# Attention and a squared-relu feed-forward: who issues the last stores, batch three's queries by the DMA crossbar, and another order

## The chip, the cores and the metric

The kernel runs on one core of a Trainium2 chip. The metric is the device time of one execution in microseconds. Besides it there is one profiled execution, with its own time, from which all rows below come.

## The reference

```python
q, k, v: (8, 8, 576, 64); p: (8, 8, 32, 64)              # batch, heads, sequence, head dimension
def sm_attn(qq, kk, vv):
    s = matmul(qq, kk.T) / sqrt(64)
    a = exp(s - max(s)); a = a / (sum(a) + 1e-9)
    return matmul(a, vv)
p_packed = sm_attn(p, k, v)                              # 32 packed rows per head
attn = sm_attn(q, p_packed, p_packed)                    # (8, 8, 576, 64)
x = attn.transpose(0, 2, 1, 3).reshape(4608, 512)
out = square(maximum(x @ w_in, 0)) @ w_out               # (512, 2048), (2048, 512): float32 (4608, 512)
```

## The kernel before, in words

**Work.** The eight batches (b) go through the same steps. k, q and v are loaded in halves of four heads (Lk, Lq, Lv; GpSimd issues these loads, which also cast to bf16). k is transposed by DVE (Tk), v is put in place by DVE (Cv, two halves, each after all four pieces of Lv of that batch). S1 gives the scores of the packed rows, PV the packed rows (XT takes them out of PSUM: a copy, a reciprocal, and two small copies into `pq`, `pq_part` or `pq_swap`). M multiplies the packed rows with `w_in`, so that the second attention and the first feed-forward matmul become one (R: 16 matmul steps per batch, each followed by a relu on ACT or DVE; F1: squares into `gT`). S2 and N are the scores and the normalisation of the second attention; S2 needs the transposed queries `qT`.

**Queries.** In batches that aren't in `XBAR`, DVE transposes the queries (`tr_q`, line 275). In batches in `XBAR`, SP issues a DMA transpose of each half from SBUF to SBUF (Tq, `xbar_q`, line 281), `s2_x` takes 16 matmuls in place of 32 (line 413 in place of 430), `pq_swap` stands for `pq_part`, and the output rows of that batch are stored in another order. `qT` has two buffers.

**Second feed-forward matmul.** The 36 output tiles of 128 tokens (F2) are done one by one up to tile 6 and for tile 35; tiles 7 to 34 go in seven groups of four (`GROUPS`), named by their first tile. A group computes the four tiles' halves by seven products of sums and differences (F2.g.n.kk: product n of 1 to 7, eight steps kk), with WS the sums of `gT` on DVE and `prod_out` the copies and additions from PSUM into `o_sb`. Products 1, 3, 5 and 7 share one bank, so product 3 starts when product 1 has been copied out. `o_sb` has three buffers: a new one can be written when all stores of the tile pair three back have landed.

**Stores.** ST.t (or ST.g.6 for tiles g and g+1, ST.g.7 for g+2 and g+3) stores a tile in two pieces of two DMAs, each of 32 rows. Every piece may go by SP, from tile 8 on by GpSimd, and from tile 31 on by ACT:

```python
for e, us, eng in (("SP", 0.86, nc.sync), ("POOL", 1.0, Q), ("ACT", 0.86, A))
if e == "SP" or t >= (8 if e == "POOL" else 31)]
```

**Order.** Steps are cut into pieces. `ORDER` is a packed list with one number for each piece: which of its allowed engines does it, and its place in one list over all engines. `Plan.run` unpacks it and issues the pieces in that order; each engine then works its own pieces strictly in that order, and a piece whose data isn't there holds all behind it on its engine. This includes SP, which issues stores and crossbar transposes, and GpSimd, which issues loads and stores. `FILL` gives, for some early steps, how many idle matmuls TensorE does ahead of them (`keep_clock`). The names used below (Lv.6.0.0, Cv.6.0, XT.5, ST.4) are step names: kind, batch or tile, and piece. Line 1024 is the barrier behind the kernel, line 541 the stores, 226 to 247 the loads of q, k and v, 172 and 170 copies by DVE and ACT.

Of the kernel before, what the change touches and what calls it, by code (L numbers as in the profile page):

```python
# [76 lines left out]
ORDER = (
    'c-jrt17j5m7y!`EVd3s-)mm;DtJSit)t23smR2phwrsm)+qP}nw)x(#I0rx=2_%A~kP{3NLssyC<d6rFfg6H>At7V}FQkRy;0t~b0;wS*l!E+F'
    '0IESQ2!cvb1}Z``C<$dD9I8Vd=mQO)IgEx*&<z$sD`*chpfc2iE>Ig9!VstcRiQ16fU$5G2E$0$3QZsqCPGgb0IOjEEQM>Z9M-`tm;jUEEKGyh'
    'a0xcUPIv@2;2tEvy>JNLzzH}9-{B5C1t&g+*N_HZzz4{Tf<9OQ^I#$DitpeH1fv^MV_p0Tf1wzb#!A==t6(i0h&8c3j>kaEjV*C8uEmp>5wl@q'  # L80
    'oPi5)54ORMxEkl<ay)=f@eL9+$F?{ZH{x!*hVStQ`cX~_p_cRtKcX*9!CAN&SK<~thei%6Lf`NYrls_hjj9n-BFamXXcn!cxwM!zQYy+smFW>a'
    '!w)!?rqB|q%}sd#XQ3c!K-IY}_vQf3#QC`ix8k8ZgXYsZy2RJ{F_+=0+?p$KICtjJG=XMPDo)2a_zK_Q_gsieazif0<+wR#<Gfs%GjdKY$_NS$'
    'AV>iIkPb39(mMhn3uJQ?0w=h@11F&<6oXgr9!B6;{EEM^EA^*j?B=PwjO$5PNdYM#4Wx1eIL<>NOo=-%DV?QBoEdUJFSr6Vurpr5JNOS%6R`3k'
    'KE;(KO7cQ^Xbdet(Tg*2116*jRFSGuZ>mXkr~_@GU38ST(>}UD-}oOVl0S@+N|K6O0>vd>36kuP8}dOBC<uk21eAtyPzA!Eh9eYi!hN_4Pv9B6'
    'gpcqUe!?#YVKM~Y_Sgmc-~{ZCgK#>o!cDl<_Yj`K`@RqG2|mZq_zr&|l2Bqw?krB_ojGU~ZK5@Fg7(r8I!EW}GF_otbc3EyPwvb8c@z)gaXgu)'
    '@C=^C3wXY39%qvrl1qw9J}DxlrL2^f3hpqeDOKG^<+vP^Q*v5v%L92VPvyD$wY-xz?pjb6>N)zsFo=aUupTx#w!jY9?O=3ZDh$PT*Z?2n3*VQR'
    'm5Nb5I!>pYr|BBqcHW^rJdlU*7@o+}IlJVS+)_+RNg4MEIVYFpt~_)<l6KlzJ9_%)AkP4;4^5#FL_lk32OXg$w1E!L8KNK>x<U+ehe0qLdO&aJ'
    '4{?wIb72+?!6H}<Yhz(7i(%LVe<F~QliZYn3Xq5VDLa*<<+PgC(^lF+7wH3Sqy6-VUeQZ>L!ame{U+vm{F9JVZ~<P*>v#ok;qAPikMTC%!$<fQ'
    '*OB_tR9Z?K=_iAwqjZ*$vQ$cH8Lg^~w5hh&?%F~lHA?$xUl`~Z3ZoojV7y}-OoAye(=i?9z<gK?OJD_ThkbAmj=~W*1!v$gT!5=^9UeL!z*~3@'
    'pB&w=H}=53z5{SL4#8144yWNnoQLta6qn&TT#vhOJMPDWcoYxgaXgLZ@d94PD|j7m;BBlzH7JzAsV+69Ce*?iNm0~}qNxjYqwds)`q3a7OmWU('  # L90
    'G=fIbIGRY)XgbZId9;8Q(o!N$$O$+JCuJ9VIHfB!r{@fug|l-I=i`E0m`ibKuE15e7Kd?tZp@L~lB2jCcjQhS!~6K4>oA|-lYEBH@&&%kH~1z$'
    ';79y|U-BD%$DjEN|Kh)_Vv<;rh_5)sPy8jVJB_55*3w?ONH^&ry`_)zcMp^y5-Y=Ggp6~Kmx(e}X38v?C-Y^IES6=mLRQNfSua~;hwPNS@>V{$'
    '-^&;Gcljm1<)5&ciYC@1np_>~Qjezc_-lZs(~O#3b7@`;)&g2s!?mu~)&@F4N9!mZ>zSaFb&^iknL0=3>T+GCt9703)-Af%b4<_a1-<OKsyFnO'
    '-qrj1NFVD{eW9;BQz0H!!8W)Ex8Vnv?_ivSD{vnk!LxW1A7UeFPd#ZMjiRZvh*nTq4&*#sf@^RKj^<u`o}ch5{>mZ_$tYQ+mrRx!GFKMLI@u#f'
    'B$4{6pC_~C)M8pro9jHC@7d%zqSy6~KG%;r4;H~nSPQ#g5A25n@DCDVI!uq5FgxbOd{_Wy!CY7d8(<S0gX3@-{s3Z8EQL|n38OIv`{6hE4T&)c'
    'CdK6Fi!StFR?LC<u?$wkde{&n&<|6fKL%i0%!%c&Dptoj*a(|qGi-s8*c!WI5EjJZSRPwp2kePnil?=-fi}}_I!Mpx8+GS?JeXs71W(|Nyp>Z*'
    'PRT35Qb=k`b7>{p<fNRD3vyNN$q)G>q^e0ZpBB{WI$THURGp;@b*XOEQ~FcE5}VunExl#6oL1e!Z6uDtIk*tF;a)t3C-4kj#H)A<@8Ugtjc+lt'
    '^Amo-@AwxJkPjuHWaOe0l#&7{4W*-u6iBt4c_=>xQ$Z?BMX3apqS92B%26e%PGMA=8d7s=MiJDCI#Oqfp<dLNVrc*kp`kRK#?W}0OtWbj?W8?)'
    'fDX}NIz}hy3|*&7bd_$>UAjm2=>a{Y7xb8((sO!EZ|NPqr;qfDKGPTaO5f=Z{iS~-oS2Ohu@5`h%l@2(Gjn-YR?f}A9Kyx9ELY@e+}2fx8*npj'
    '!yUK_cjF#Bmg9IB59g6Qn#c1rp2>@OHqYU?9M21R2`}fByxO&j*YH|i&l`9XZ{{7mi+A#F-pdF05Fh2^e44NFIljo(_%=V}r~I1V@(0%^{>i_Y'  # L100
    'C8798GVw@iNg)A}PBKU)$t+nUkCc!CQcyyquoRV&QcfyL4XGqmq?%NhP^l&1Qdb(e8%RTGEKQ`Dw2%milupuC+DQkAmKf<SJ*BS<l>stH;$*mt'
    'k_j?Nrpqe#Y>AfzvP724N?9u#<dAHY-Lg;i%K<qoXXU)yl#6mnuE;gHE;r<s+>!h8M4rhDc`2{tqkNLj@=d<VPx&kVqpt}xq57y-lc`hPnnF`*'
    'YE7eQHN9rgOd6;;G`Hs05G|smJVmv*meA5#R?BN;t)jKGn%2-z4bysBUmI#;ZKcgLLR)HUZKG|qgLcxM8m(QltHx+I?V-K2xAxQiI#37e5RKJ1'
    '9je20qK?sVI$o#fG@YTdHC|Wh0$rqwb&0OfRk}vk>SoV2-KBeUpYGR#dRUL@2|c4{^}JrxD|$_D>TP|X_w=DY(P#QnU+WuvtMB!le$Y?)S-<F4'
    '{ifgbm;TV-`bYojKm9+0#-=7_mcSBPBJ;5%mei74GIN-(In8ArOKGVrz*1WpOJ^A@qXk+v%Wk<Whvl{)%V+s5*a})9D`JJMs1>skR?<pYX)9yp'
    'tgMx{3Rcl7S!JtYRjr0qvrwyPwJgkPTOF%w^{t*Yu!h#i8e0=<YR#;LHMa<hw3gP&T3dVTV4ba_b+TydVlmdux?2zHX}zqU^|t{w$Oc=i4YxQO'
    'Y9nl<jk3`;#>U$On`o14icPg?Hr-~}EGvN}u`-5ZERM!uI2Ge?GS0>&I20G*8r+GwC^r?NGE|S6QhjPmt*H%lq8^l-9qh-sT)wU%9LhDhy{i#N'
    'xVrLPe(t)*&-lLUBY$TQa{q88kmNF2#<-`sr^r~DBO7It>~e3H&F+JeMYC!)Pmm{%7Sak@QEPfCdFptY=z86t+jXPofS%MHdfIcyv(s~2FR9lG'
    'n4hJ!6yD;N$+B1;%k0hT4Y4-XHn6KV%G!B{Sa0iN1HF9%hXqcyu{O>-(>u>*+Z>x47;papcrZuK'
)  # L110
# [918 lines left out]
```

## Time and profile before

| | |
|---|---|
| time, median of 11 runs | 249.9 us (246.49 to 253.19) |
| the profiled execution | 247.79 us, span 246.0 us |
| TensorE (PE) busy | 226.1 us, 92% of the span |
| DVE, ACT, GpSimd (POOL) busy | 180.9, 158.9, 89.4 us |
| last matmul ends, by the timeline | 237.7 us |
| stores issued by SP, GpSimd, ACT | 82, 58, 8 DMAs |
| crossbar transposes | 8, issue 1.3 to 4.8 us each on SP |

The span runs from the first to the last instruction of the profiled execution; 1.8 us of its time lie around it. A line of the profile names the source line, the engine, the operation and the tiles, then either the count and the mean time, or, in a timeline, start, length, and in brackets the engine's idle time before it with what ended it. POOLq, SPq and ACTq are instructions that the engine's queue handles itself, such as issuing a DMA.

### The profile page before, as it was taken

How to read it: one execution, taken by the hardware profiler on the slowest of the kernel's cores; microseconds unless marked ns; L12 is line 12 of the kernel's file. 1: busy time of each engine (PE TensorE's matmuls, PEld its weight loads, DVE VectorE, ACT ScalarE, POOL GpSimd, SP SyncE). 2: the span in 40 equal slices, each digit the busy share in tenths (PEclk: the TensorE clock that was granted, in tenths of full speed). 3: DMA queues.
4: the chain of work that ended last, by engine and by line, in shares of the span. 5: the costliest groups of instructions: out<-in, count | busy, mean ns of one | idle time of the engine just before them, and what ended most of it. 6: DMA issues, size and time to landing. Idle time of an engine off the chain costs nothing.

```text
span 246.0 us, 6016 instructions
## 1 busy us (share of the span) xinstructions
PE 226.1 (92%) x2417; PEld 172.6 (70%) x2417; DVE 180.9 (74%) x315; ACT 158.9 (65%) x265; POOL 89.4 (36%) x177
## 2 busy tenths in 40 slices
...
DMA  6999999999999994089952960131005004106070
GB/s 221 177 208 203 197 199 208 203 228 224 234 205 222 181 189 86 3 149 196 213 79 51 186 131 0 24 102 51 1 12 148 17 0 118 57 3 171 0 210 6
DMA packets 35708, 31.43 MB, mean 128 GB/s; under 512 B 15232, under 2 KB 28160, under 8 KB 35680
## 3 DMA queue, kind: packets, MB, share of 16 engines
...
q8 instruction: 19, 0.31, 0.5%
...
## 4 chain that ended last, share of the span: by engine, by line
PE 69%; DMA 20%; DVE 3%; POOL 3%; issue 2%; ACT 1%; POOLq 0%; DVEq 0%
PE ps_o L620 31%; PE ps_h L470 19%; DMA w_in_b<-in_moe_w_in_dram 7%; DMA v_r<-in_v_dram 7%; PE ps_o L561 6%; DMA q_b<-in_q_dram 6%; PE ps_a L561 3%; PE ps_m L383 3%; PE ps_pp L331 2%; PE ps_a L296 1%; PE ps_s L444 1%; POOL out_dram L541 1%; PE ps_s L430 1%; PE ps_s L413 1%; PE ps_o L547 1%
## 5 line engine op out<-in xcount | busy, mean ns | idle before, releaser
L499 ACT ACTIVATE r<-ps_h 128x576 bf16<-128x576 f32 x97 | 62.6, 651 | 19.7 <-PE ps_h L470 17.6
L470 PE MATMUL ps_h<-a,M 128*128 128x288 bf16 x448 | 71.7, 286 | 0.1
L541 POOL DMA_DIRECT2D out_dram<-o_sb x58 | 28.7, 502 | 101.8 <-DVE o_sb L633 91.9
L510 DVE TENSOR_TENSOR gT<-r 128x1152 bf16<-128x1152 bf16 x60 | 44.7, 751 | 12.9 <-ACT r L499 10.1
L470 PEld LDWEIGHTS <-M 128*128 128x128 bf16 x448 | 43.7, 98 | 11.0 <-issue 0.6
L620 PEld LDWEIGHTS <-wS 128*128 128x128 bf16 x448 | 42.6, 98 | 9.3 <-issue 3.2
L620 PE MATMUL ps_o<-wT,wS 128*128 128x256 bf16 x336 | 41.7, 273 | 0.4 <-DVE wS L606 0.4
L620 PEld LDWEIGHTS <-gT 128*128 128x128 bf16 x336 | 32.7, 98 | 5.6 <-issue 0.2
L620 PE MATMUL ps_o<-w_out_b,gT 128*128 128x256 bf16 x224 | 32.5, 273 | 0.0
L170 ACT COPY o_sb<-ps_o 128x512 f32<-128x512 f32 (+1 forms) x24 | 13.8, 575 | 24.8 <-PE ps_o L620 21.1
L247 POOL DMA_DIRECT2D v_r<-in_v_dram x32 | 19.3, 610 | 24.3 <-DVE v_b L172 9.9
L170 ACT CAST M<-ps_m 128x1024 bf16<-128x1024 f32 (+1 forms) x26 | 23.5, 931 | 2.0 <-PE ps_m L383 1.8
L561 PE MATMUL ps_o<-w_out_b,gT 128*128 128x512 bf16 x80 | 23.1, 380 | 0.1
L606 DVE TENSOR_TENSOR wS<-gT 128x1024 bf16<-128x1024 bf16 (+1 forms) x32 | 19.1, 617 | 0.2
L633 DVE TENSOR_TENSOR o_sb<-ps_o,o_sb 128x512 f32<-128x512 f32 x21 | 14.4, 684 | 5.1 <-issue 2.9
L561 PEld LDWEIGHTS <-gT 128*128 128x128 bf16 x112 | 10.1, 98 | 10.3 <-issue 2.0
L620 PE MATMUL ps_o<-wT,gT 128*128 128x256 bf16 x112 | 16.3, 273 | 0.0
L620 PE MATMUL ps_o<-w_out_b,wS 128*128 128x256 bf16 x112 | 15.8, 273 | 0.0
L501 DVE TENSOR_SCALAR r<-ps_h 128x576 bf16<-128x576 f32 x15 | 11.3, 756 | 5.9 <-PE ps_h L470 5.9
L458 DVE SCALAR_TENSOR_TENSOR a<-e,rD,ls 128x576 bf16<-128x576 bf16 (+1 forms) x18 | 13.0, 744 | 3.1 <-ACT ls L452 3.1
L438 ACT ACTIVATE e<-ps_s,rD 128x576 bf16<-128x576 f32 (+1 forms) x18 | 11.4, 684 | 4.8 <-PE ps_s L430 2.8
L172 DVE CAST M<-ps_m 128x1024 bf16<-128x1024 f32 (+1 forms) x10 | 10.6, 1064 | 4.3 <-PE ps_m L383 2.8
...
## 6 DMA issues: line engine op xcount, KB each, us to landing
out_dram<-o_sb SPq DMA_DIRECT2D x80, 64.0 KB, 3.0
...
out_dram<-o_sb POOLq DMA_DIRECT2D x54, 64.0 KB, 2.5
...
```

What stands on the lines that cost most here:

```text
L170: nc.scalar.copy(dst, src)
L247: nc.gpsimd.dma_start(self.vr[32 * i:32 * i + 32, h0:h1, :n * D], src[:, :, J0[i] * D:(J0[i] + n) * D])
L438: nc.scalar.activation(self.e2[qd, hf], self.pss[qd, hf], ACT.Exp, scale=self.rD[:, qd:qd + 1])
L458: nc.vector.scalar_tensor_tensor(out=self.a2[:, qd, n0:n1].rearrange("p (c n) -> p c n", n=HALF), in0=self.e2[qd, hf], scalar=self.rD[:, q ...
L470: nc.tensor.matmul(ps[:, c, :HALF], lhsT=a.M[:, qd, fb * FB:(fb + 1) * FB], rhs=a.a2[:, qd, c * HALF:(c + 1) * HALF], start=(qd == 0), sto ...
L499: nc.scalar.activation(dst, src, ACT.Relu)
L510: eng.tensor_tensor(out=dst, in0=r, in1=r, op=ALU.mult)
L541: eng.dma_start(dst, src[32 * i:32 * i + 32])
L561: nc.tensor.matmul(po[t], lhsT=gT[:, fb, n0:n0 + P], rhs=w_out_b[:, fb, :], start=(fb == 0), stop=(fb == NFB - 1))
L606: eng.tensor_tensor(out=dst, in0=a, in1=b, op=op)
L620: nc.tensor.matmul(ps[:, u * EH:(u + 1) * EH], lhsT=lhs, rhs=rhs, start=(n in (1, 2, 4) and kk == 0 and u == 0), stop=(kk == KB - 1 and u ...
L633: eng.tensor_tensor(out=o, in0=ps, in1=o, op=ALU.add)
```

## The change

Three constants and the rule for the stores' engines are changed, and `ORDER` is another list:

```diff
-XBAR = (4, 5, 6, 7)
+XBAR = (3, 4, 5, 6, 7)
...
-FILL = {'S1.0.0': 31, 'S1.0.1': 4, 'PV.0.0': 12, 'M.0.0': 16, 'N.0.0.0': 11, 'S2.0.1': 3, 'N.0.0.1': 10, 'R.0.0': 1, 'R.0.2': 3, 'R.0.1': 4, 'R.0.4': 2}
+FILL = {'S1.0.0': 30, 'S1.0.1': 13, 'PV.0.0': 12, 'M.0.0': 9, 'N.0.0.0': 6, 'S2.0.1': 2, 'N.0.0.1': 9, 'R.0.0': 1, 'R.0.2': 3, 'R.0.1': 4, 'R.0.4': 1}
...
 ORDER = (
-    'c-jrt17j5m7y!`EVd3s-)mm;DtJSit)t23smR2phwrsm)+qP}nw)x(#I0rx=2_%A~kP{3NLssyC<d6rFfg6H>At7V}FQkRy;0t~b0;wS*l!E+F'
+    'c-jrt17j5m7y!`Ex$dsAYqhj&uC~0etYv%4ZfkL?Eo<4fZQHhOzjuDc0T4(EK9CZMfI(u&0f`_P<bmYign~ej5Yj>tNCE!ffecU*(m_@TfZ|XF'
...
                         for e, us, eng in (("SP", 0.86, nc.sync), ("POOL", 1.0, Q), ("ACT", 0.86, A))
-                        if e == "SP" or t >= (8 if e == "POOL" else 31)]
+                        if e == "SP" or (8 <= t < 31 if e == "POOL" else t >= 27)]
```

Unpacked, the two lists differ in these places. A piece is two DMAs for a store, one for a load.

- **Stores at the end.** Of the twelve pieces of tiles 31 to 35, GpSimd issued five, ACT four and SP three; now SP issues six and ACT six. GpSimd's last stores are one piece of tile 28 (ST.27.6) and one of tile 30 (ST.27.7). ACT takes one piece each of ST.27.6 and ST.27.7, ahead of the copy F2.31.1.7.
- **SP's list, tiles 1 to 6.** Before: ST.1, 2, 3, 4, Tq.4.0, Tq.4.1, ST.5, ST.6, Tq.5.0, Tq.5.1. Now: ST.1, 2, 3, Tq.3.0, Tq.3.1, Tq.4.0, ST.4, ST.5, Tq.4.1, ST.6, Tq.5.0, Tq.5.1. Further on Tq.6 and Tq.7 both stand ahead of ST.11.6; they stood after its pieces and between those of ST.11.7.
- **GpSimd's list.** Lv.6.0.1 and Lv.6.0.2 come right behind Lv.6.0.3, ahead of Lk.7.1, Lv.5.0.2, X.6 and ST.7.6; they came after the first piece of ST.7.6. Behind ST.7.6 (both pieces) now come Lv.7.0.3, Lq.6.1, Lk.6.0, Lv.7.0.2, Lq.7.1, Lq.7.0, and then Lv.6.0.0. Lv.5.0.1 and Lq.5.1 come ahead of Lv.4.0.1; they came after it. The 28 loads up to the last piece of Lv.1 are the same ones in another order.
- **DVE's list.** Tq.3.0 and Tq.3.1 are gone. Cv.4.0 stands behind F1.2.7, and behind it come F1.2.9, Cv.4.1, F1.2.11, WS.7.1.0, F1.2.13, F2.7.1.7, F1.2.15, WS.7.1.1, WS.7.2.0. Cv.6.0 still stands ahead of XT.5.
- **TensorE's list.** Between R.2.15 and S2.3 there are now four steps of product 2 of group 7; before there was none. Elsewhere neighbours change places.
- **Engines.** Some thirty copies, relus and squares change between DVE and ACT; DVE has 270 pieces in place of 275, ACT 267 in place of 260.

More of the change, by code (lines that the diff above doesn't have):

```diff
@@ L72, in run @@
             fn()
-FILL = {'S1.0.0': 31, 'S1.0.1': 4, 'PV.0.0': 12, 'M.0.0': 16, 'N.0.0.0': 11, 'S2.0.1': 3, 'N.0.0.1': 10, 'R.0.0': 1, 'R.0.2': 3, 'R.0.1': 4, 'R.0.4': 2}
+FILL = {'S1.0.0': 30, 'S1.0.1': 13, 'PV.0.0': 12, 'M.0.0': 9, 'N.0.0.0': 6, 'S2.0.1': 2, 'N.0.0.1': 9, 'R.0.0': 1, 'R.0.2': 3, 'R.0.1': 4, 'R.0.4': 1}
 ORDER = (
-    'c-jrt17j5m7y!`EVd3s-)mm;DtJSit)t23smR2phwrsm)+qP}nw)x(#I0rx=2_%A~kP{3NLssyC<d6rFfg6H>At7V}FQkRy;0t~b0;wS*l!E+F'
[L79 to L109, printed above, removed]
@@ new lines @@
+    'c-jrt17j5m7y!`Ex$dsAYqhj&uC~0etYv%4ZfkL?Eo<4fZQHhOzjuDc0T4(EK9CZMfI(u&0f`_P<bmYign~ej5Yj>tNCE!ffecU*(m_@TfZ|XF'
+    'YJ)HMK{Y4^<)J=QgeuS(szMzY1RbCo%z+@N3E|Ka`oUtT3r%1YG=vr~0m?xjw1ROk5sp9vjE5c24BEgH7zo2*Ei8l;a2;Y{Dx8HGFdr_%YS;vK'
+    'U>od(M{pA!fZ#qj3~%8ST!gQ151xV(AH!?Nh>6e#i(op;iVd+i2H;?1OpJN)A1LO)6qpLDV0O%n?Xe<O!x5MtOJZ-Vi%oDMHpZ4X8@-qTYvT&s'
+    'j0dn4cEW|&1N-7~e1K2z3vR$2cmlWKKD>en$VoY<Ce@?9bP!MB3tWt=aVPG^LwE<vP#`s>0IEi9C^O}y^2C&gQd4qDO9g2;t*5<|lCn_=I*AwY'
+    '4f;_bszv#^IM?JVRGYd|Wv<Nwc{;_@YMMifX#>U4Oj<<MIfRFEE-t|3xg&SyI9^DrXfxH}#vH|sxFwJ0qFjcXa1PGPCAb1t<sMv;D{^Z_P;dZ4'
@@ new lines @@
+    '0>}axAroYF<bvFeyp96k0=L5pr=cuVfLHJi#^EIVfqyWPCQ@R~!i#w;H<Nyn3er2WL25@DxCAfZGfc+<be$G(cE}H5a1B~uINrd=sFaGFoR)9#'
+    'J#HjnQV5Ddb7&2S9-N8m@Gzdnf0%?^G>F`kp2kxb>On_oHyxtOw4aXCLz=*oc`i@lX}pFH^C`Z>$N4Nj;GB>T3PTAf2Bo1AREFwM1L{FA)N<U0'
+    '`*0VYz%zIO@8J`CgYS+%kPOYI8}`CM7>mPjB+kHPxE?q99KrMW+~*~}#dr7(KjCjA5=u-y&fFC2^reloleW-VI!PDl2Hm7PbeG=KBYHw3IFd*6'
+    '93IOvcp)$1WxRsd@&?y>&L{b$pj42eQdR<`vQ(97?qCUV*K(hf({f7A$z{1OPvn)nk+<$|^1=OGLZA^eb_|9n7y)Zw18j9{hh4DSL6{noVjb*)'
+    'P4P9p_xXVNsS=f>3v`99I`7kS=TnN{F&xdacs?&>e<>z~q`U;VE6EwTB-iDkJas>l?%K-}u0u7_Gg2EsQwW8Y&=xvDS7-<Ap$qhYj?f)?L2u{-'
@@ new lines @@
+    '!(cS@h5j%EMnX39$DCLKOJhx}kEJjWL$Cw>LL?&(rJ;OOl)RLc3R78HN1JFn?V$s7i+<5QIzeyf3w@?P^o^K}Q*b*LPQux^5^v$Xyq%Bm3BJrv'
+    '_#~g_8~m0VN)u@%9i+1imr>GFdP}q{kpQi&RkWqH)*d=Q+i3^wro(gq40S}p7#IsN5Dk+c4yHS%!7P{ui(mmPgFSEn4#H751}ESooP+al1+Kyk'
+    'cnELcIedUVI1u~e5TD^V79(*2#^5xZf^%^mF2W_a3fJOx+=6>?KOV=Ucor|<RlJ5b@fP02d-w?JP<;xa#?I!{l0vDivpsd9&eW57Q5c0&e;P<b'
+    'XedR{C>ld!DTXG|WST-VXco<*`LvXhv5S2;4X5KwoSCz`{5T)`b73yVWw{&&aup8dT3nwSaws?Dw%mccayRb9;oRRffQRr!zUsQpcla(p<VXCJ'
+    'pYtnz&F}aFf95azi~leRiAh39ArA3KN=YMWC4*#^?CxxmLpn+~=_CDRpbU|rGQu4pQ8HS_$pndWPnM}NQ|3y%ER@BvOqR<kStILZgKU!>vPbsG'
```

17 lines of the change are left out of this document (added).

## The prediction

> **What bounds the kernel now.** I read the page first (shares, then the slices), then the table of busy time by stretches, then the waits and the timelines of the three places where TensorE stands still, and last the records of the barrier behind the kernel.
>
> ```profile
> span 246.0 us, 6016 instructions
> PE 226.1 (92%) x2417; PEld 172.6 (70%) x2417; DVE 180.9 (74%) x315; ACT 158.9 (65%) x265; POOL 89.4 (36%) x177
> DMA  6999999999999994089952960131005004106070
> ```
>
> TensorE is busy 92% of the span, and the DMA engines are full in the first 14 slices (to about 86 us) and again from about 98 to 120 us. Up to 38 us the chain of waits runs through loads. From there matmuls follow each other densely, so an edit pays only where TensorE stands still, or behind its end.
>
> ```profile
> 80.00:100.00 20.00, 19.27 (x254) 14.48 (x253) 16.41 (x27) 16.07 (x26) 2.69 (x6) 1.00 0.80 141
> 120.00:140.00 20.00, 18.07 (x192) 14.96 (x191) 13.84 (x26) 14.05 (x22) 6.56 (x15) 1.00 0.62 103
> 220.00:246.00 26.00, 17.67 (x162) 15.59 (x160) 7.49 (x12) 3.30 (x6) 7.83 (x16) 0.88 0.34 92
> ```
>
> The columns are the stretch, its length, and busy us of PE, PEld, DVE, ACT and POOL (clock and DMA last). TensorE loses 0.7 us in the first row, 1.9 in the second and 8.3 in the third, where the last matmul ends at 237.7.
>
> **Part 1, the last stores.** The records of the closing barrier (line 1024) show what the end waits for:
>
> ```profile
> L1024 SPq EVENT_SEMAPHORE  x11: 17/28/28, 239.7 to 246.0; - x11
> L1024 POOLq DRAIN  x3: 46/98/7188, 238.1 to 245.8; - x3
> L1024 SPq DRAIN  x3: 7/7/13, 241.8 to 245.5; - x3
> ```
>
> GpSimd's first drain starts at 238.05, when it has issued its last store, and takes 7.19 us: to 245.24. SP, which waits for every store to land, has its drain at 241.88. So the drain holds the end for 245.24 - 241.88 = 3.4 us, and 0.75 us of barrier follow. The other two drains, with no store just issued, take 0.05 and 0.10. In the changed order GpSimd's last store is one of tiles 29 and 30 (ST.27.7), which the trace has at 222.9: a drain of the same 7.2 us from 224 ends near 231, under TensorE's last 6 us. If the drain were not over by then, up to 3.4 us come back.
>
> Against this stand ten more issues by SP and ACT. The tail (tiles 31 to 35) has 24 stores; now SP issues 6, ACT 8, GpSimd 10; then SP 12 and ACT 12.
>
> ```profile
> 233.18 5.99 SPq L541 DMA_DIRECT2D out_dram<-o_sb  x6
> 234.83 3.00 ACTq L541 DMA_DIRECT2D out_dram<-o_sb  x4
> 238.00 0.37 ACT L170 COPY o_sb<-ps_o 128x256 f32<-128x256 f32 x1 [3.20 <-DMA out_dram<-o_sb]
> DMA to landing us min/median/max: 1.6/3.4/4.0
> ```
>
> An issue takes 0.31 to 0.99 us, about 0.42 usually: 12 x 0.42 = 5.0 us from 233.2 is 238.2, no later than the last copy. But the records also show that SP and ACT share eight semaphores in turn, so a store waits until the eighth before it has landed (ACT's store at 237.00 follows a landing at 236.98). 24 stores are three rounds, and on ACT the last copy (F2.35.1.15) stands behind the second-round and third-round stores. With landings of 2.0 to 2.7 us, as in the bursts at 184 and 205, the third round goes out at 237.4 and the copy slips about 0.4 us; with the 3.4 to 4.0 of this burst it slips 1.5 to 2 us. Bounds: gain 3.4 (no slip), loss 1.9 (12 issues of 0.99 each, 245.1, plus the shortest landing and 0.4 us of SP's waits, against 245.24). The usual issue is nearest to the first: I take a gain of 2.6. ACT also takes a store of tile 28 and one of tile 30 ahead of the copy F2.31.1.7 (four issues, 1.7 us, from about 222); TensorE needs that copy at 225.3, where product 3 of the group starts: nothing, and up to 1 if the stores' data came later.
>
> [...]
>
> **Part 2, queries of batch three by the crossbar.** Two DVE transposes go (2 x 1.35 us, row L275), and two pq_part of 0.69 and 0.75 become pq_swap of 0.28 and 0.30. That is 3.6 us of DVE and ACT work off engines that are not the bound: nothing by itself. S2.3 becomes 16 matmuls instead of 32, and four F2 products now stand between R.2.15 and S2.3:
>
> ```profile
> 89.33 0.28 PE L430 MATMUL ps_s<-qT,pp 32*32 32x288 bf16 x1
> 90.00 0.28 PE L430 MATMUL ps_s<-qT,pp 32*32 32x288 bf16 x1 [0.40 <-ACT r L499]
> ```
>
> Between its first and second matmul S2.3 waits for a relu that frees its bank. It holds TensorE 1.29 us (89.33 to 90.62); S2.4, of the new form, holds it 0.37. Gain 0.9.
>
> Its price is on two queues. SP gets two transposes, ahead of Tq.4.0 and of the stores of tile 4, which stood before them:
>
> ```profile
> L275 DVE STREAM_TRANSPOSE qT<-q_b x10: 736/1341/1378, 9.5 to 75.2; 128x1152 bf16<-128x1152 bf16 x6, 128x576 bf16<-128x576 bf16 x4
> L281 SPq DMA_TRANSPOSE qT<-q_b x8: 1297/1652/4823, 74.7 to 142.8; - x8
> DMA to landing us min/median/max: 3.2/4.4/12.3
> ```
>
> Tq.3.0 can go when ST.3 is out (61.3) and its load has landed (64.0), Tq.3.1 when its load has (71.4), then Tq.4.0. In this stretch an issue took 2.4 and 4.8 us, so ST.4 goes out at about 71.4 + 2.4 + 4.8 = 78.6, a little over 80 with later loads, instead of 72.9. ST.5 behind Tq.4.1 landed 6.1 us after issue; so ST.4 lands at 86 to 91. Its o_sb slot (three of them) goes to F2.7.1.7, which in the new DVE order stands behind F1.2.13, at about 90: just covered. Batch three's queries land at 84 to 87, before S2.3 near 89.
>
> The other queue is the DMA engines, full until 86 us. A crossbar transpose keeps all 16 busy for about 1.9 us (the packets of the four around 78 to 96 us sum to 7.8), so two are 3.9 us more work there. Lv.4.0.1 also goes behind two more loads (Lv.5.0.1, Lq.5.1: 0.8 and 1.4 us by the spacing of landings). It already ends a wait:
>
> ```profile
> 82.64 0.49 DVE L172 COPY v_b<-v_r 128x1280 bf16<-128x1280 bf16 x1 [1.45 <-DMA v_r<-in_v_dram]
> ```
>
> I estimate its landing at 86.6 (82.6 + 2.2 + about 1.8 of the 3.9). DVE then stands before Cv.4.0 from about 83.6, with F1.2.9, Cv.4.1, F1.2.11, WS.7.1.0, F1.2.13, F2.7.1.7, F1.2.15, WS.7.1.1 and WS.7.2.0 behind it: 6.3 us at the rows' 0.5 to 0.76 each, so F2.7.3 starts at 92.9 instead of a possible 91.5. Loss 1.4; bounds 0 (the load lands as before) and 4.4 (all 3.9 us and a slow load ahead of it, 89.6).
>
> [...]
>
> **Part 3, the other order.** The largest wait inside the dense part is this one:
>
> ```profile
> 104.41 1.12 POOL L541 DMA_DIRECT2D out_dram<-o_sb  x2 [9.35 <-DVE o_sb L633]
> 116.43 0.60 POOL L247 DMA_DIRECT2D v_r<-in_v_dram  x1
> 123.93 0.49 DVE L172 COPY v_b<-v_r 128x1280 bf16<-128x1280 bf16 x1 [3.40 <-DMA v_r<-in_v_dram]
> 124.81 0.09 PEld L413 LDWEIGHTS <-pp 64*32 64x32 bf16 x1 [2.18 <-DVE pp L172]
> ```
>
> GpSimd sits before a store of tile 8 until 104.4, with loads behind it; the last of batch six's v is issued at 116.4 and lands at 123.7. DVE waits for it in Cv.6.0, XT.5 stands behind that, and S2.5 behind XT.5: TensorE reaches S2.5 at 122.75, starts at 124.81 and loses another 0.3 inside. In the new order Lv.6.0.1 and Lv.6.0.2 are issued before that store, and Lv.6.0.0 after four stores and six loads: at 0.8 to 1.4 us a load, it lands near 118, ahead of Cv.6.0 (119.9). Gain 2.4; bounds 2.4 and 0 (the load still late). The two loads that go ahead now also stand before X.6 on GpSimd; they wait for Cv.4.1 (about 88), X.6 for S1.4.2 (93): nothing.
>
> The start: the same 28 loads stand ahead of Cv.1, whose last piece lands at 37.3 and ends the chain there; fewer fill matmuls (97 to 90) and swaps between DVE and ACT lie before it. Nothing, within 0.5 either way. Other swaps after 40 us touch engines with slack: nothing; TensorE's remaining small waits (about 2 us in all) could shrink or grow by 1.
>
> **Sum**, against the profiled execution (247.79 us: span 246.0 and 1.8 around it): -2.6 - 0.9 + 1.4 - 2.4 = -4.5, span 241.5, that execution 243.3. The median before, 249.9, is 2.1 above the profiled one, and I carry the difference over: **245.4 us**.
>
> **Rivals.** *The mid wait stays* (Lv.6.0.0 late again, as GpSimd still sits before tile 8's store): without 2.4 the change is -2.1, 247.8. For it: its issue is still behind that store. Against: far fewer loads ahead of it. *The tail gives nothing*: either the drain's length isn't tied to GpSimd's last store, so that the change doesn't do what it says, or the semaphore rounds take its place: -1.9, 248.0. For it: GpSimd's stores had all landed by 240.7, so the drain isn't just that. *All gains, no new wait*: -3.4 - 0.9 - 2.4 - 1 = -7.7, 242.2. *Slower: ST.4 behind the crossbar.* If the three transposes ahead of it go down SP's ring one after the other at the worst row's 12.3 us from 61.3, they end at 98.2, ST.4 lands at 100, F2.7.1.7 to WS.7.2.0 take 2.8, and F2.7.3 starts at 102.8 instead of 91.5: +11.3 - 5.9 = +5.4, 255.3. It turns the sign once ST.4 lands after 91.5 + 5.9 - 2.8 = 94.6. Against: the two transposes at 74.7 and 77.2 ended within 1 us of each other.
>
> **Chances.** Forecast 0.52 (its own range 243.5 to 247.4), all gains 0.14, mid wait 0.13, tail 0.11, slower 0.10. This kernel's measurement tells about 1% (2.5 us) from no change. Faster takes the first two and 0.03 of the mid wait's: 0.69; same has the rest of mid wait and tail: 0.21; slower 0.10. The range runs from 241.5, just under the best case, to 250.5, past both cases of one missing gain, with the slower case left out above.
>
> **What would show it.** Right: a POOL drain that starts near 224 and ends before 232, with SP's drain last; no wait of PE at L413 near 122; Cv.6.0 without a DMA wait. For the loss: Cv.4.0's wait at DVE over 2 us. Wrong: a POOL drain still last; ACT's last copy after 239.5 by this trace's clock; F2.7.1.7 waiting for a store's landing; S2.3 waiting for qT.

## The result, and the profile after

| | before | after |
|---|---|---|
| time, median | 248.64 us (47 runs, 246.49 to 253.19) | 252.2 us (12 runs, 249.63 to 256.45) |
| the profiled execution, its span | 247.79, 246.0 us | 251.31, 249.5 us |
| granted clock of TensorE, mean | 0.987 | 0.975 |

The ratio is 1.0139 with a 95% interval of 1.0101 to 1.0177: the change makes the kernel 1.4% slower, where 1.8% less than the first median was forecast. Ratios leave out executions that took over 1.5% longer than the fastest of the same kernel beside them; medians have all of them.

The page and the table of busy time by stretches after the change (stretch, length, busy us of PE, PEld, DVE, ACT and POOL, clock, DMA share):

```profile
span 249.5 us, 5970 instructions
PEclk9999999999999995699999999999999999999998
```

```profile
80.00:100.00 20.00, 9.76 (x103) 7.65 (x101) 8.31 (x14) 10.28 (x17) 4.49 (x8) 0.84 1.06 183
100.00:120.00 20.00, 19.84 (x216) 15.10 (x217) 16.38 (x29) 12.92 (x21) 7.68 (x17) 0.90 0.50 82
120.00:140.00 20.00, 19.35 (x236) 15.47 (x235) 17.58 (x32) 15.61 (x25) 5.20 (x12) 1.00 1.16 191
220.00:249.50 29.50, 25.18 (x230) 22.19 (x227) 13.65 (x22) 5.15 (x8) 1.97 (x4) 0.96 0.30 81
```

From 80 to 100 us TensorE lost 0.7 us before; now it loses 10.2. The slices of the clock show 5 and 6 there, and 0.90 still stands in the next stretch. From 120 to 140 us, where 1.9 us were lost, it is 0.65. So the loss sits in one place, and the gains elsewhere are real. The start of the same TensorE step in both traces gives the account:

| TensorE step | before | after | difference |
|---|---|---|---|
| R.1.0 | 52.71 | 51.15 | -1.6 |
| R.2.0 | 76.55 | 75.25 | -1.3 |
| S1.4.0 | 90.62 | 87.91 | -2.7 |
| M.3.0 (after F2.7.3.0 to .5) | 94.03 | 103.26 | +9.2 |
| S2.4 | 99.03 | 108.61 | +9.6 |
| F2.15.1.0 | 136.10 | 143.60 | +7.5 |
| F2.35.1.15, the last matmul | 237.40 | 244.90 | +7.5 |
| end of the span | 246.0 | 249.5 | +3.5 |

Between S1.4.0 and S2.4 the change costs 12.3 us; everything else together (-2.7, -2.1, -4.0) gains 8.8.

The waits from 75 to 105 us, longest first, lines left out (engine, tile and line that waited, what released it, us in all, times, longest):

```profile
DVE v_b L172 <- DMA v_r<-in_v_dram: 11.3, 1, 11.3
...
PE ps_o L620 <- DVE wS L606: 10.4, 1, 10.4
POOL k_b L226 <- DMA qT<-q_b: 9.3, 1, 9.3
```

These three are links of one chain, and it starts at the last. The timelines of GpSimd, SP's queue, DVE and TensorE, in the order of the chain:

```profile
61.42 21.51 SPq L281 DMA_TRANSPOSE qT<-q_b  x3
```

```profile
75.64 0.53 POOL L226 DMA_DIRECT2D q_b<-in_q_dram  x1 [2.38 <-DMA qT<-q_b]
85.45 1.06 POOL L226 DMA_DIRECT2D k_b<-in_k_dram  x2 [9.28 <-DMA qT<-q_b]
86.49 0.61 POOL L247 DMA_DIRECT2D v_r<-in_v_dram  x1
```

```profile
93.89 0.49 DVE L172 COPY v_b<-v_r 128x1280 bf16<-128x1280 bf16 x1 [11.34 <-DMA v_r<-in_v_dram]
```

```profile
100.16 1.46 PE L620 MATMUL ps_o<-wT,wS 128*128 128x256 bf16 x6 [10.41 <-DVE wS L606]
```

k and q share eight buffers. Lq.4.1 takes the one that Tq.3.0 reads, Lk.5.0 the one that Tq.3.1 reads. A buffer that DVE transposes from is free when DVE is done (before: Tq.3.1 ended at 76.60, and the load that took its buffer, Lq.5.1, went at 76.89); one that the crossbar reads is free when the transpose has landed. Tq.3.0 landed 13.7 us after its issue, at 75.11; Tq.3.1, issued at 73.4, at 84.92. Lq.4.1 goes at 75.64 and Lk.5.0 at 85.45, each 0.53 us after the landing that it waits for. The list of GpSimd's changes given with the change leaves out one move that counts here: Lk.5.0, which was issued at 64.66, ahead of Lv.5.0.0, now stands behind Lq.4.1, two places ahead of Lv.4.0.1. So GpSimd issues Lq.4.1, waits 9.28 us with Lk.5.0, issues Lk.6.1, and only then, at 86.49, the last piece of batch four's v, Lv.4.0.1 (73.6 before). It lands at 93.86 instead of 82.62. DVE waits for it in Cv.4.0, the sum WS.7.2.0 stands nine pieces behind that copy, and TensorE waits for it before F2.7.3. After it the clock is low, 0.50 from 94 to 104 us: from F2.7.3.0 to M.3.0 TensorE takes 3.10 us where it took 1.63, and from M.3.0 to the next product 0.91 where it took 0.56, 1.8 us more in all. From there to S2.4 it takes as long as before.

The closing barrier (line 1024), the lines that answer to those of before:

```profile
L1024 POOLq DRAIN  x3: 46/102/5385, 231.2 to 249.3; - x3
L1024 SPq DRAIN  x3: 7/7/7, 248.7 to 249.0; - x3
```

GpSimd's long drain starts at 231.2 and ends at 236.6, under TensorE's last products, and SP's is the last. From the start of the last matmul to the end of the span it is 4.6 us instead of 8.6.

### The profile page after: what moved, and what is told of

Same layout as the page of the kernel before. It is cut to its first block, busy times and chain, and to the rows that moved or that the text cites. A ratio compares the mean times of both kernels' runs of the same rounds, so it can differ in the third digit from the quotient of the medians.

```text
span 249.5 us, 5970 instructions
## 1 busy us (share of the span) xinstructions
PE 227.5 (91%) x2394; PEld 172.4 (69%) x2394; DVE 177.2 (71%) x308; ACT 160.7 (64%) x266; POOL 79.7 (32%) x157
## 4 chain that ended last, share of the span: by engine, by line
PE 60%; DMA 25%; DVE 6%; POOL 3%; issue 2%; ACT 2%; ACTq 0%; DVEq 0%; POOLq 0%
PE ps_o L620 33%; PE ps_h L470 17%; DMA q_b<-in_q_dram 8%; DMA v_r<-in_v_dram 5%; DMA qT<-q_b 5%; DMA p_b<-in_p_dram 4%; PE ps_m L383 2%; DVE gT L510 2%; POOL pT_bd L172 2%; DMA p_f<-in_p_dram 2%; DMA out_dram<-o_sb 1%; PE ps_pp L331 1%; PE ps_a L296 1%; DVE wS L606 1%; PE ps_s L444 1%
## 5 line engine op out<-in xcount | busy, mean ns | idle before, releaser
L620 PEld LDWEIGHTS <-wS 128*128 128x128 bf16 x448 | 43.0, 99 | 20.8 <-DVE wS L606 11.5
L620 PE MATMUL ps_o<-wT,wS 128*128 128x256 bf16 x336 | 43.3, 278 | 11.1 <-DVE wS L606 11.1
L510 DVE TENSOR_TENSOR gT<-r 128x1152 bf16<-128x1152 bf16 x59 | 43.7, 754 | 12.5 <-ACT r L499 8.9
L541 POOL DMA_DIRECT2D out_dram<-o_sb x38 | 18.9, 502 | 99.3 <-DVE o_sb L633 87.0
L170 ACT COPY o_sb<-ps_o 128x512 f32<-128x512 f32 (+1 forms) x19 | 10.9, 573 | 20.1 <-DMA out_dram<-o_sb 13.6
L561 PEld LDWEIGHTS <-gT 128*128 128x128 bf16 x112 | 10.2, 98 | 11.1 <-issue 2.2
L172 DVE COPY v_b<-v_r 128x1280 bf16<-128x1280 bf16 x16 | 7.6, 493 | 13.8 <-DMA v_r<-in_v_dram 13.1
L501 DVE TENSOR_SCALAR r<-ps_h 128x576 bf16<-128x576 f32 x14 | 10.6, 757 | 8.5 <-PE ps_h L470 8.4
```

Source lines behind the costliest of these rows:

```text
L170: nc.scalar.copy(dst, src)
L172: eng.tensor_copy(dst, src)
L510: eng.tensor_tensor(out=dst, in0=r, in1=r, op=ALU.mult)
L541: eng.dma_start(dst, src[32 * i:32 * i + 32])
L561: nc.tensor.matmul(po[t], lhsT=gT[:, fb, n0:n0 + P], rhs=w_out_b[:, fb, :], start=(fb == 0), stop=(fb == NFB - 1))
L620: nc.tensor.matmul(ps[:, u * EH:(u + 1) * EH], lhsT=lhs, rhs=rhs, start=(n in (1, 2, 4) and kk == 0 and u == 0), stop=(kk == KB - 1 and u ...
```

## The experiments

**Theory:** GpSimd's wait for a buffer that a crossbar transpose holds delays the load behind it (head of the line). **Rivals:** the new order of the loads; the load of two more transposes on the DMA engines, whoever waits; the stores of tile 4 behind the transposes on SP (the forecast's slower rival); the clock. All edits of the order are moves in `ORDER`; they are shown as lists. Each ratio is against the kernel before, run beside it on the same chip.

| | ratio to before, 95% | median, us | before Cv.4.0, DVE waits |
|---|---|---|---|
| before | 1 | 248.64 | 1.45 |
| after | 1.0139 (1.0101 to 1.0177) | 252.2 | 11.3 |
| 1: after, batch three by DVE | 0.9866 (0.9749 to 0.9983) | 245.07 | 4.5 |
| 2: after, Lv.4.0.1 ahead of Lk.5.0 | 0.9737 (0.957 to 0.9904) | 244.0 | 2.2 |
| 3: after, Lv.4.0.1 early | 0.9817 (0.9699 to 0.9935) | 244.58 | 0 |
| 4: before, batch three by the crossbar | 1.0266 (1.0174 to 1.0357) | 254.96 | 7.7 |
| 5: before, last stores as after | 0.9899 (0.9805 to 0.9992) | 246.13 | 1.5 |
| 6: before, two loads earlier | 0.9897 (0.9858 to 0.9936) | 246.05 | 2.0 |
| 7: before, start of after | 1.0046 (0.9997 to 1.0096) | 249.77 | 3.2 |
| 8: 1 and 3 together | 0.9726 (0.9665 to 0.9787) | 240.84 | 0 |
| 10: 3, and a store ahead of Tq.4.0 | 0.9776 (0.9707 to 0.9845) | 243.58 | 0 |
| 11: 8, one late store on GpSimd | 0.9687 (0.9629 to 0.9746) | 241.29 | 0 |
| 12: 8, last copy on DVE | 0.9661 (0.9592 to 0.9729) | 240.88 | 0 |
| 14: 5 and 6 together | 0.9788 (0.9722 to 0.9853) | 242.98 | 2.4 |

**1. Batch three back to DVE, the rest of the change kept.**

```diff
-XBAR = (3, 4, 5, 6, 7)
+XBAR = (4, 5, 6, 7)
 DVE: ... Tk.4.0
+     Tq.3.0
 ...
      N.2.1
+     Tq.3.1
```

> The changed kernel with one part undone: XBAR is (4, 5, 6, 7) again, DVE transposes batch three's queries (Tq.3.0 behind Tk.4.0, Tq.3.1 behind the second N.2 product), everything else stays in the changed order, the loads too. Theory (GpSimd waits with Lk.5.0 for the q_b buffer that the crossbar transpose Tq.3.1 still reads, Lv.4.0.1 stands behind it, DVE behind that in Cv.4.0, TensorE behind that in F2.7.3): GpSimd issues Lv.4.0.1 near 78 instead of 86.5, it lands near 86.5, DVE waits 0 to 3 us in place of 11.3 and 8 to 11 us of the changed kernel's 252.2 go, less 0.9 for the 32 matmuls of S2.3: 242 to 245. Rival load order (Lq.5.1 and Lv.5.0.1, which now go ahead of Lv.4.0.1, take its time on the DMA engines): the wait stays at 8 us or more, 250 to 253. Rival clock (TensorE runs slower in the changed order for another reason): the rows from 92 to 120 us still show 0.84 to 0.90, 250 or more.

Measured 245.07 us. GpSimd no longer waits (Lk.5.0 goes at 73.6), Lv.4.0.1 is issued at 75.53 and lands at 86.71, DVE waits 4.5 us (0 to 3 were expected), and the clock is 0.91 from 80 to 100 us. Most of the loss goes with the two transposes. What is left is the rival's share: with Lv.5.0.1 and Lq.5.1 ahead of it, the load still lands 4.1 us later than before the change.

**2. One load moved by two places.**

```diff
 GpSimd: ... Lq.4.1
+        Lv.4.0.1
         Lk.5.0
         Lk.6.1
-        Lv.4.0.1
```

> The changed kernel with one piece moved by two places: Lv.4.0.1 goes directly ahead of Lk.5.0 and Lk.6.1 on GpSimd instead of directly behind them. All transposes, stores and loads stay, so the DMA engines have the same work. Theory (head of the line on GpSimd): Lv.4.0.1 is issued near 76.2 instead of 86.5 and lands at 84 to 87, DVE's wait in Cv.4.0 falls from 11.3 us to 1 to 4, and 7 to 10 of 252.2 go: 242 to 245. Rival DMA load (the crossbar transposes keep the engines from every load until 86 us, whoever issues when): Lv.4.0.1 still lands at 91 or later, and the time stays over 249. Rival stores (ST.4 behind the transposes on SP holds F2.7.1.7 by its o_sb buffer): F2.7.1.7 waits for a store instead, over 249.

```profile
75.77 0.61 POOL L247 DMA_DIRECT2D v_r<-in_v_dram  x1
85.85 1.31 POOL L226 DMA_DIRECT2D k_b<-in_k_dram  x2 [9.47 <-DMA qT<-q_b]
```

Measured 244.0 us. This is the cleanest test: the same DMA work, the same wait of GpSimd, 9.47 us long, but nothing that is needed soon stands behind it (Lk.5.0 goes 0.53 us after the landing of Tq.3.1, as in the changed kernel). Lv.4.0.1 lands at 84.75, inside what was expected, DVE waits 2.2 us, F2.7.3 starts at 91.2 instead of 100.2, and the clock from 80 to 100 us is 1.00. The DMA load alone is out as the cause: it would have kept this load late too.

**3. The load directly behind Lv.4.0.0.**

```diff
 GpSimd: ... Lv.4.0.0
+        Lv.4.0.1
         Lv.5.0.1, Lv.5.0.3, Lk.5.1, Lq.5.1, X.5, Lq.4.1, Lk.5.0, Lk.6.1
-        Lv.4.0.1
```

> The changed kernel with Lv.4.0.1 directly behind Lv.4.0.0 on GpSimd, nine places earlier. Theory (head of the line on GpSimd): it is issued near 69 and lands at 77 to 80, ahead of Cv.4.0 (near 82.5), so DVE's wait of 11.3 us is gone altogether, TensorE comes to F2.7.3 near 89 to 91 instead of 100.2, its clock stays at 1.00 behind that, and 11 to 12 us go: 240 to 242, faster than both kernels; each load behind it is 0.6 us later. Rival DMA load: another load or a transpose lands late instead, Cv.4.0 or S2.3 waits for it, 246 or more. Rival stores: F2.7.1.7 waits for ST.4's landing, over 249.

```profile
89.02 0.69 DVE L172 COPY o_sb<-ps_o 128x512 f32<-128x512 f32 x1 [2.21 <-DMA out_dram<-o_sb]
```

Measured 244.58 us, above the 240 to 242 of the theory. Cv.4.0 waits no more (82.47), but the next wait is there at once: DVE's copy F2.7.1.7 waits 2.2 us for the landing of tile 4's stores, and F2.7.3 starts at 91.8. That is the forecast's slower rival, worth some 2 us and not 11.

**4. The crossbar for batch three alone, on the old order.**

```diff
-XBAR = (4, 5, 6, 7)
+XBAR = (3, 4, 5, 6, 7)
 SP: ... ST.3 (first piece)
+    Tq.3.0
     ST.3 (second piece)
+    Tq.3.1
     ST.4
```

> The kernel before with batch three's queries by the crossbar alone: Tq.3.0 and Tq.3.1 on SP behind ST.3, ahead of ST.4; loads, DVE's list and the tail as before. Here Lk.6.1 takes the q_b buffer that Tq.3.1 reads, and Lv.4.0.1 stands directly behind Lk.6.1. Theory (head of the line on GpSimd): Lk.6.1 waits until Tq.3.1 lands at 83 to 87, Lv.4.0.1 lands near 93 instead of 82.6, DVE waits about 10 us in Cv.4.0, and with 0.9 gained in S2.3 the time is 248.6 + 6 to 11: 254 to 260. Rival load order: the order is that of before, so 247 to 250. Rival DMA load alone (two transposes more, 3.9 us of all engines): 1 to 4 us later, 248.5 to 252.

GpSimd, DVE and TensorE of this run:

```profile
78.23 0.56 POOL L226 DMA_DIRECT2D q_b<-in_q_dram  x1 [8.33 <-PE ps_h L470]
```

```profile
89.06 0.49 DVE L172 COPY v_b<-v_r 128x1280 bf16<-128x1280 bf16 x1 [7.71 <-DMA v_r<-in_v_dram]
```

```profile
92.02 1.12 PE L470 MATMUL ps_h<-a,M 128*128 128x288 bf16 x4 [6.27 <-DVE r L501]
```

Measured 254.96 us, 2.7% slower: one part of the change is enough. The place was expected wrongly: not Lk.6.1 but Lq.4.1 waits, 8.3 us, for the buffer that Tq.3.0 reads. The row names TensorE as the releaser; the transpose was issued at 64.73 and landed 12.9 us later, at 77.7, and the load went at 78.2. This is a case in which the profile names the engine that came last and the DMA was what held. Behind Lq.4.1 stand X.5, Lv.5.0.3, Lk.5.1, Lk.6.1 and then Lv.4.0.1, which is issued at 82.35 and lands at 89.04.

**5. The last stores alone, on the old order.**

```diff
 ST.31.6, ST.31.7, ST.35.0: five pieces
-    GpSimd
+    SP (three), ACT (two)
```

> The kernel before with only the stores of the last tiles changed: the five pieces of tiles 31 to 35 that GpSimd issued go to SP (three) and ACT (two), so SP and ACT have six each. GpSimd's last stores are then those of tile group 27, near 222 to 226. Theory (GpSimd's drain of some 5 to 7 us behind its last store held the end by 3.4 us): the drain runs from near 226 to 233, under TensorE's last products, SP's wait for the last landing ends the program, and 2.6 to 4 of 249.5 go: 245.5 to 247. Rival store queues (12 stores each on SP and ACT end no earlier than the drain did): 248 to 250, with the last copy on ACT later than 239.5. Rival fixed drain (its length isn't tied to a store just issued): the drain is still last, 249.5.

```profile
L1024 POOLq DRAIN  x3: 46/98/6467, 223.7 to 242.2; - x3
```

Measured 246.13 us, a gain of 1.0% (95%: 0.1 to 2.0). GpSimd's long drain starts at 223.7 and takes 6.5 us, SP's drain is the last at 241.6, and from the start of the last matmul to the end it is 5.5 us instead of 8.6.

**6. The two loads of batch six alone, on the old order.**

```diff
 GpSimd: ... Lv.6.0.3
+        Lv.6.0.1
+        Lv.6.0.2
         Lv.5.0.2, X.6, ST.7.6, Lv.7.0.0
-        Lv.6.0.1
 ...
         Lk.6.0
-        Lv.6.0.2
```

> The kernel before with two loads moved on GpSimd: Lv.6.0.1 and Lv.6.0.2 directly behind Lv.6.0.3, ahead of Lv.5.0.2, X.6 and the stores of tiles 7 and 8. Theory of part 3: batch six's v has landed before Cv.6.0, DVE's 3.4 us wait there and TensorE's 2.2 us wait at S2.5 go, nothing else changes: 249.5 - 2 to 2.4 is 247 to 247.5. Rival: Lv.6.0.0, still behind tile 8's stores, lands as late as Lv.6.0.2 did: 249 to 250. Rival given back: the gain is lost to a later wait, and the time is 249.

```profile
120.00:140.00 20.00, 20.00 (x222) 16.47 (x222) 15.99 (x30) 15.76 (x26) 5.75 (x12) 1.00 0.58 111
```

Measured 246.05 us, a gain of 1.0%. TensorE is busy without a break where it lost 1.9 us. From S2.4 to S2.5 it takes 2.0 us less than before, and to F2.15.1.0 2.3.

**7. The start alone, on the old order.**

```diff
-the first 254 places of ORDER and FILL, as before
+the same of the changed kernel, then the rest in the old order
```

> The kernel before with the changed kernel's start: its first 254 places (to about 40 us: order of the first 34 loads, swaps between DVE and ACT) and its counts of fill matmuls, everything behind it in the old order. In the changed kernel's trace TensorE is 1.1 to 1.6 us ahead from the first relu steps on. Theory (that lead comes from the start's order): 248 to 248.4 instead of 249.5, the lead seen from R.0.0 on. Rival (the lead comes from the order behind it, or is run to run): 249 to 250, R.0.0 where it was.

```profile
82.69 0.49 DVE L172 COPY v_b<-v_r 128x1280 bf16<-128x1280 bf16 x1 [3.17 <-DMA v_r<-in_v_dram]
```

Measured 249.77 us: no gain. Yet the lead is there: R.1.0 starts at 51.04 instead of 52.71, R.2.0 at 74.88 instead of 76.55. It is given back in one place. Lv.4.0.1 lands when it landed before, Cv.4.0 starts at 82.69 instead of 82.64, and DVE merely waits 3.17 us for it instead of 1.45. S1.4.0 is where it was (90.67). Both halves of the expectation were half right.

**8. Both repairs: batch three by DVE, and Lv.4.0.1 early.** The edits of 1 and 3 in one kernel.

> The changed kernel with both repairs: batch three's queries by DVE, and Lv.4.0.1 directly behind Lv.4.0.0. With DVE's transposes alone Lv.4.0.1 was still issued behind Lq.5.1, Lv.5.0.1 and three more, landed at 86.7, and DVE waited 4.5 us (245.1 us). Theory (order of the loads is the rest of it): it lands at 77 to 79, that wait goes, TensorE's clock stays at 1.00 in 80 to 100 us, and 2.5 to 4 us go: 241 to 242.5. Rival (something else then holds DVE or TensorE there, such as the store of tile 4 or Tk.4): 244 to 246.

Measured 240.84 us (240.71 to 242.46), 2.7% under before: the version that beats both kernels. Cv.4.0 and S2.5 don't wait for loads, F2.7.3 starts at 89.94. With the crossbar kept, 2 and 3 have much the same spans in their profiles (239.2 and 239.9 against 239.1) and overlapping intervals, but medians over 3 us longer; that the crossbar itself costs something more isn't settled.

**9 and 13. The copy later on DVE.** In the first try Cv.4.0 and Cv.4.1 went behind WS.7.2.1 and so, in the program, behind three loads of batch six into the same buffer. They then wait for these loads and put batch six's v in place of batch four's (Cv.4.0 at 105.2, 253.45 us). That says nothing on the question. In the second these loads went behind the copies too.

```diff
 DVE: ... F1.2.7
-     Cv.4.0
      F1.2.9
-     Cv.4.1
      F1.2.11, WS.7.1.0, F1.2.13, F2.7.1.7, F1.2.15, WS.7.1.1, WS.7.2.0, WS.7.2.1
+     Cv.4.0
+     Cv.4.1
 GpSimd (13 only):
-     Lv.6.0.3, Lv.6.0.1, Lv.6.0.2
      Lk.7.1, Lv.5.0.2
+     Lv.6.0.3, Lv.6.0.1, Lv.6.0.2
```

> The changed kernel with Cv.4.0 and Cv.4.1 moved on DVE, from behind F1.2.7 and F1.2.9 to behind WS.7.2.1: eight pieces that TensorE needs sooner no longer stand behind the copy that waits for Lv.4.0.1. GpSimd's order and its wait stay, so Lv.4.0.1 still lands near 94. Theory (the stall reaches TensorE by DVE's order): DVE goes on to WS.7.2, F2.7.3 starts at 90 to 92 instead of 100.2, PV.4 has its v_b near 95, about where it is wanted, and 8 to 11 of 252.2 go: 241 to 245. Rival (TensorE would have been held by PV.4 all the same, since v_b is late for it): the wait moves from F2.7.3 to PV.4 and only 2 to 5 us go, 247 to 250.

> The changed kernel with Cv.4.0 and Cv.4.1 on DVE behind WS.7.2.1, and the three loads of batch six that overwrite what these copies read (Lv.6.0.3, .1, .2) behind them in the program, so behind Lk.7.1 and Lv.5.0.2 on GpSimd. GpSimd still waits with Lk.5.0, and Lv.4.0.1 still lands near 94. Theory (the stall reaches TensorE by DVE's order): DVE does F2.7.1.7 near 89 and WS.7.2.1 near 92 and only then waits, F2.7.3 starts at 91 to 93 instead of 100.2, PV.4 waits little, and 6 to 10 of 252.2 go: 242 to 246. Rival (v_b is late for PV.4 anyway): TensorE stands still before PV.4 for 7 us or more, 249 to 252.

TensorE of 13:

```profile
90.83 0.83 PE L620 MATMUL ps_o<-wT,wS 128*128 128x256 bf16 x6 [1.38 <-DVE wS L606]
101.34 0.39 PE L331 MATMUL ps_pp<-e,v_b 128*128 128x64 bf16 x4 [7.71 <-DVE v_b L172]
```

F2.7.3 is free at 90.83, as the theory said, and TensorE then stands 7.7 us before PV.4, as the rival said. The median of four runs is 252.03, but they spread from 247.6 to 252.5, and in the profiled one Lv.4.0.1 landed only at 100.8; no ratio can be formed, and how much the move is worth stays open. Had the load landed at 93.9, as in the changed kernel, PV.4, which TensorE reaches near 94, would hardly have waited; why it landed later here isn't shown. What the run shows is that the order on DVE chose which product stood still, and that the move helps only as far as the load lands by about 94.

**10. A store of tile 4 ahead of Tq.4.0.**

```diff
 SP: ... Tq.3.1
+    ST.4 (first piece)
     Tq.4.0
-    ST.4 (first piece)
     ST.4 (second piece)
```

> The changed kernel with Lv.4.0.1 early, and on SP the stores of tile 4 ahead of the transpose Tq.4.0 (behind Tq.3.1) instead of behind it. With Lv.4.0.1 early alone, DVE's copy F2.7.1.7 waited 2.2 us for a landing of tile 4's store (its o_sb buffer), and F2.7.3 started at 91.8. Theory (that is the forecast's slower rival, worth little once the 10 us are gone): ST.4 goes out near 76 to 78 and lands before 86, that wait goes, F2.7.3 starts near 90, 1 to 2 us less than with Lv.4.0.1 early alone (244.6): 242 to 243.5. If batch three's crossbar has no other price, this comes to the 240.8 of the kernel with both repairs and DVE's transposes, less up to 0.9 for the short S2.3: 240 to 241.

Only one of the two pieces went ahead in the list, so the edit is half of what was expected of it. It still shows what the place is worth: that piece was issued at 75.88, not 84, and landed at 87.05, a quarter of a microsecond behind the transpose Tq.3.1 (86.80). F2.7.1.7 waited 2.0 us, F2.7.3 started at 91.5, and 243.58 us can't be told from 244.58. The second piece, behind Tq.4.0, landed at 88.55 (Tq.4.0 at 88.14), and that is what F2.7.1.7 waited for. A store behind a transpose in SP's list lands just behind it in these traces (0.25 and 0.41 us here, 0.17 us behind Tq.4.0 in the changed kernel, 0.19 us behind Tq.4.1 before), so I estimate that both pieces ahead of Tq.4.0 would still land after 86.8 and bring about 1 us at most.

**11. One store back on GpSimd, in the kernel of 8.**

```diff
 ST.35.0, first piece (two DMAs)
-    SP
+    GpSimd
```

> The kernel with both repairs (240.8 us, span 239.1), and one piece of ST.35.0 (two small DMAs) back on GpSimd, which has no other store of tiles 31 to 35. Theory (GpSimd's drain takes its 5 to 7 us behind a last store, however few came just before): the store is issued near 232.5 to 233.5, the drain ends at 239 to 241, up to 2.5 us behind SP's drain at 238.2, and the time is 241 to 243.5. Rival (the drain's length grows with the stores still under way, here two): a drain of 1 to 3 us, hidden, 240 to 241.

```profile
L1024 POOLq DRAIN  x3: 46/102/5705, 232.6 to 238.8; - x3
```

The drain is 5.7 us long behind two small DMAs, as in the kernel of 8 behind its last store of tile 30, so its length doesn't come from the stores just issued. In all the traces it goes with the number of stores that GpSimd issued in the whole kernel: 7.2 to 7.3 us with 58, 6.5 with 48, 5.3 to 5.7 with 38 or 40. Why isn't shown. Here it starts at 232.6 and ends at 238.3, together with SP's (238.2). So it costs little or nothing here: 241.29 us is at the low end of what was expected and can't be told from 240.84.

**12. The last copy on DVE, in the kernel of 8.**

```diff
-("ACT", 0.38, lambda: f2_last_out(1, A))
+("DVE", 0.38, lambda: f2_last_out(1, V))
```

> The kernel with both repairs (240.8 us, span 239.1), and the last copy out of PSUM (F2.35.1.15) on DVE instead of ACT. On ACT it stood behind stores that wait for one of the eight shared semaphores: it began at 235.38, though the last matmul ended near 233.1. Theory (third-round stores hold the copy): on DVE it begins near 233.2, the last two stores go when a semaphore is free, near 235.0 instead of 235.8, and 0.5 to 1 us go, 239.8 to 240.4. Rival (the semaphores' rounds hold the last stores all the same): 240.5 to 241.

ACT's copy in the kernel of 8, which this edit is after:

```profile
235.38 0.37 ACT L170 COPY o_sb<-ps_o 128x256 f32<-128x256 f32 x1 [10.36 <-DMA out_dram<-o_sb]
```

On ACT the copy begins 2.5 us after the start of the last matmul (232.85); on DVE 0.3 us after it (235.64 against 235.33, a later start in that trace). From the start of the last matmul to the end it is 5.8 us instead of 6.2, and the time, 240.88 us, is the same. The rival holds: with the copy on DVE done at 236.06, SP and ACT still issue stores until 238.6 and 238.5. That they wait for the rounds of the semaphores is the reading of the changed kernel's records, where ACT's store at 243.50 goes on the semaphore of the eighth store before it, which landed at 243.48.

**14. Parts 1 and 3 together, on the old order.** The edits of 5 and 6 in one kernel.

> The kernel before with parts 1 and 3 only: the five pieces of the last stores from GpSimd to SP and ACT, and Lv.6.0.1 and Lv.6.0.2 earlier on GpSimd. Alone, the first took 1.0% and the second 1.0% of the time, with spans of 242.5 and 244.3 against 246.0. Theory (they sit in different places and add up): span 240.5 to 241.5, the time 2% below before, 243.5 to 245. Rival (one gives back the other, as the earlier end of TensorE meets the same landings of the last stores): 245.5 to 247.

Measured 242.98 us, a gain of 2.1%, span 241.1 against 246.0: 2.3 us by the last matmul (235.11 against 237.40) and 2.6 us behind its start. The two add up.

## Why the prediction was wrong

**The step that failed** is the loss of 1.4 us in part 2, "bounds 0 (the load lands as before) and 4.4". It measured 12.3: 10.5 us by the later start of F2.7.3 and 1.8 us of slow clock behind it. The landing of Lv.4.0.1 was put at 86.6 by adding DMA work to the old landing, with the time of its issue left at about that of before. It was issued 12.9 us later. For that issue time the estimate was not bad: issued at 75.5 to 75.8 in experiments 1 and 2, the load landed at 86.7 and 84.75. The work on the DMA engines was priced and the two queues, SP's and the DMA's, were walked; the third, GpSimd's, was walked only for what was moved in it, not for what each of its pieces waits for. The buffer was named nowhere in the sum.

The trace of before had the hint. In its waits from 60 to 95 us stands

```profile
POOL q_b L226 <- DVE qT L275: 2.1, 1, 2.1
```

so a load of GpSimd already waited for the reader of a q buffer: Lq.5.1, issued at 76.89, when DVE had ended Tq.3.1 at 76.60. Handing that reader to the crossbar, whose landings the forecast itself quoted at 3.2 to 12.3 us, made such waits 2.38 and 9.28 us long in the changed kernel, for whichever load took the buffer next, and delayed everything behind it on GpSimd too.

**The clock** was left out of the price of a stall. After 10.4 us without a matmul TensorE takes 3.10 us for what took 1.63; after experiment 1's 3.2 us it takes 2.60; after the 1.3 and 2.0 us of experiments 2 and 3 it takes 1.63. Behind the 10.4 us the granted clock is 0.50 from 94 to 104 us and 0.99 from 104 to 106, and the slow stretch costs 1.8 us; from 80 to 100 us it is 0.91 in experiment 1 and 1.00 in experiments 2 and 3. Experiment 1's stall already cost 1.6 us up to S2.4. At what length of stall the slow clock sets in isn't shown.

**The slower rival** had the right sign and near the right size (255.3) by the wrong link. It was to turn the sign once the stores of tile 4 landed after 94.6; they landed by 86.7, and F2.7.1.7 followed DVE's list without a wait of its own. Its link exists, though: experiments 3 and 10 show it at 2 us, and in experiment 10 the stores land right behind the transposes.

**Part 1** was right, and a little small: forecast 2.6, measured 4.0 in the changed kernel, 3.1 in experiment 5, 2.6 in experiment 14. The drain moved as forecast. The spread comes from the semaphore rounds, for which the forecast gave two cases: in the changed kernel's trace SP's and ACT's stores use eight semaphores in turn, the first round landed in 1.7 to 1.95 us and the last copy began 0.86 us after the start of the last matmul (0.60 before); in the kernel of experiment 8 most of the first round took 3.4 to 3.7 us and the copy began after 2.53. The 4.0 passes the bound of 3.4, as with faster landings SP's wait was shorter too: the last store landed 1.67 us after its issue (2.67 before). Experiment 5, which changes only who issues these stores, measured 1.0%.

**S2.3** took 0.37 us (87.54 to 87.91) as forecast, but most of that gain is the new order's: with batch three on DVE and 32 matmuls (experiments 1 and 8) S2.3 doesn't wait inside either and takes 0.62 us. The crossbar's own part is 0.25 us. **Part 3** was right: the forecast was 2.4, and from S2.4 to F2.15.1.0 it brought 2.1 in the changed kernel and 2.3 in experiments 6 and 14. **The start** was put at nothing within 0.5; in this pair of traces TensorE was 1.3 to 1.6 us ahead from 51 us on. Some of that is run to run: the five traces with the old start reach R.1.0 at 51.7 to 52.9 us, nine of the eleven with the new one at 51.0 to 51.4. Experiment 7 has the lead and shows it to be worth nothing with the load of Cv.4.0 landing where it did. In the kernel of experiment 8, whose Cv.4.0 doesn't wait, the last matmul starts 2.3 us earlier than in experiment 14; the lead is part of that, but the two differ in more.

With 1.4 us for the loss, the measured gains (4.0 + 2.7 + 2.1) would have given 7.4 us. Experiments 2 and 3, the changed kernel with that one load moved, are 1.8 to 2.6% under before.
